# Attention and expert kernel on one core: finishing h from the maxima, gate divisors on GpSimd, and a new planned order

## The chip, the cores and the metric

The kernel runs on one core of one Trainium2 chip. The metric is the device time of one execution in microseconds. It was 238.63 us as the median of three runs, between 236.97 and 240.13.

## The reference, cut to what matters

There are 4 batches (B) of 11456 tokens (N) with 128 channels (C), and 32 inducing vectors (m). A first attention gathers each batch's tokens into 32 vectors h, a second one gives each token a mixture of its batch's h. Then every token is sent to one of 8 experts.

```python
scale = 1.0 / np.sqrt(C)
def mab(q, kv):
    s = scale * (q @ kv.transpose(0, 2, 1))
    s = s - s.max(-1, keepdims=True)
    a = np.exp(s)
    a /= a.sum(-1, keepdims=True) + 1e-09
    return a @ kv
h = mab(I, x)            # I: the inducing vectors, (B, 32, 128)
x = mab(x, h).reshape(B * N, 128)
xn = x / (np.linalg.norm(x, axis=-1, keepdims=True) + 1e-06)
logits = xn @ en.T / tau                 # en: 8 normalized expert vectors
expert_idx = np.argmax(logits, axis=1)
probs = softmax(logits)                  # with 1e-9 in the divisor
gate_w = probs[np.arange(N), expert_idx]
out = gate_w[:, None] * (relu(x @ w1[expert_idx]) @ w2[expert_idx])
```

## The kernel before, in words

**Stages.** A batch is cut into 6 pieces k: five of 2048 tokens and a last one of 1280 that laps over 64. All pieces of one batch go through these steps.

- `load_xT` and `load_x` (L382, L394) bring the piece in two layouts, channels by tokens (`xT`, 7 buffers; the last piece `xL`, 2) and tokens by channels (`x`, 6 half pieces). They are issued on SP's queue. For pieces 0, 1 and 3 of batch 0 the second layout is not loaded: `own` (L439) makes it on PE by transposes and copies it into a buffer of the output ring `o`.
- `stage1` (L462) is the first attention: scores on PE (L425), maximum over the row on DVE (L485), running maximum `nb` (L492, L494), exponentials on ACT (L500), the correction factor `fix` (L505), the running sum `zs` (L511), transposes on PE (L523), copies (L530), products with x on PE (L546) and the running h, `hj` (L556, L558). Batch 0 does it piece by piece, the others in pairs of pieces.
- `finish` (L562) makes h from them. The 128 partitions hold four groups of the 32 rows, each with a maximum of its own. The maxima are turned into one row (L570), their best per row is found (L575, L580), turned back (L584, L589), and gives a factor `fw` for each partition (L594); the sums are weighted with it (L600) and added over the groups (L604); from the inverse comes the matrix `sel` (L609 to L614), and one product with `hj` gives h transposed, `hT` (L620, L621, L626). `tables` (L680) makes what the gates need of h. Then the expert of the batch's h is picked (L639 to L646), and SP reads its index and loads that expert's two weight matrices (L674).
- `stage2` (L699) is the second attention for a piece: scores (L716), maximum over 32 rows (L722), spreading (L727), difference (L733), exponentials `e` (L738), a product for the squared norm (L744, copied at L750, multiplied on GpSimd at L754, summed at L758) and the products for the logits (L766, L767, turned at L774).
- `gate` (L780) takes three pieces together (the last batch 3, 2 and 1; nine gates in all): the norm's root on ACT, Newton's step on GpSimd (L825 to L828), the divisor `den` on DVE (L834, L835), logits on GpSimd (L840), their maximum (L845), subtraction (L849), exponentials on ACT (L854), their sum `se` on GpSimd (L864 to L866), the first maximum `v` on DVE (L871, L873), and `f` on DVE, the gate weight where the chosen expert is the batch's (L886 to L888). `zz` (L814) is the attention's own divisor.
- `fold` (L898) makes from the weights and h one matrix `L` per batch, which replaces the expert's two layers where no hidden unit changes its sign within the batch. `check` (L973) tests that.
- `stage3` (L1056) spreads `f` (L1042), weights `e` with it on GpSimd (L1046), multiplies with `L` on PE (L1065), copies to the output buffer `o` (L1072, 2 buffers) and stores it from ACT's queue (L373).
- `worklist` (L1098) lists what the tests left open; a loop at the end does that work in full. Its list is empty for these inputs.

**The order.** Nothing is scheduled by hand. Each step is an operation given to `Plan` (L102) with its engine, an estimated duration, what it depends on, which buffers and PSUM banks it takes and frees, and a due time `when`. `Plan.run` (L198) simulates the five engines in order: among the operations of an engine that can start within a margin (`NEAR`, L79) of the earliest it takes the one with the smallest `when` plus a correction by name (`FIRST`, L62; in the last batch also `LATE`, L70). Batch 0's first stage has due times below zero, then batch b's second stage runs with batch b+1's first. The order so found is the order in which the instructions are emitted; an engine works through its own in order, and so does a DMA queue. `HOP` is the assumed delay from one engine to another, `RATE` the assumed DMA rate in bytes per us.

**Zero products.** Where the plan sees PE idle for over 0.6 us before an operation that takes a bank, it puts products of zeros there (`fill`, L1153, its product in L1157), in that operation's own bank.

Of the kernel before, what the change touches and what calls it, by code (L numbers as in the profile page):

```python
# [44 lines left out]
NC = E + 1  # L45
# [16 lines left out]
FIRST = dict(G=-52.5, at=28.5, chk=-3, chosen=60, copy_s=47, den=23.5, diff=10, em=-60, evict=55.5, ex=-44, expA=21, expB=-30, expert=59,  # L62
             f=-59.5, fin=-58.5, first=-23, fix=8, flags=-11, fours=-5, fw=-44.5, gat=6, get_w=-10.5, get_x=53, get_xT=-48.5, gm=-38.5,
             gm4=-30, gmb=-12.5, good=-60, gv=-11.5, hT=8.5, hTc=-5.5, hb=-4.5, hj=55.5, hs=35.5, keep_e=23, keep_hq=-21, keep_x=-60,
             lg=-60, li=-16.5, lm=-47.5, mat=14.5, merge=8, mk=5, mults=-3, nb=51, newton=1, norm=-44, outs=34, parts=-21, pick=-47.5,
             pick_vals=46, places=39, prod=-2, put_h=54, put_li=-7.5, put_o=-30.5, r1=22, rm=60, root=8.5, root_e=23, rows=-5,
             score=-59.5, scores=-7, se=-2, seen=44, selr=-12, sides=-3, signs=52.5, some=-52, spread=-60, spread_f=14, square=-57.5,
             square_e=-9, squared=18.5, sums=4, times=36, top=58.5, turn=-31, turn_e=-52, turn_s=1.5, under=-37.5, vals=60, vp=-10.5,
             vpb=-14.5, weigh=60, zf=44, zs=38.5, zz=-60)
LATE = dict(G=1.5, L=-7, at=27.5, chk=48.5, chosen=-60, copy_s=60, den=14.5, diff=-31, em=35, evict=49.5, ex=34, expA=14, expB=1,  # L70
            expert=2.5, f=2.5, fin=-7, first=-60, fix=60, flags=-22.5, fours=56, fw=8, gat=28.5, get_w=60, get_x=21, get_xT=52, gm=56,
            gm4=60, gmb=-60, good=25, gv=-48.5, hT=-20, hTc=-31, hb=-60, hj=21, hs=52, keep_e=52.5, keep_hq=-58, keep_x=-43, lg=13.5,
# [1245 lines left out]
```

## Time and profile before

| what | value |
|---|---|
| median of three runs | 238.63 us |
| the profiled execution | 236.28 us |
| its span, first to last instruction | 234.5 us |
| mean granted TensorE clock | 0.905 |
| instructions | 5142 |
| busy PE, DVE, ACT, POOL | 198.0, 179.4, 118.2, 108.0 us |
| moved by DMA | 72.24 MB, 308 GB/s over the span |

The span is that of the instructions; 1.8 us of the profiled execution lie outside it. PE is TensorE's matrix product, PEld its loading of weights, DVE VectorE, ACT ScalarE, POOL GpSimd, SP the engine that issues most loads. "L754" is line 754 of the kernel. In a group of instructions, "hq<-hq,e" names the tile written and the tiles read; "x24" is the number of instructions. "A <- B" with a time is A's idle time until B released it. PE's busy time has modelled ends and overlaps in part, so a high share doesn't say that it works at its peak.

### The profile page before, as it was taken

The page shows a single profiled execution, that of the slowest core. Times are in us where ns is not written, and L with a number is a line of the kernel's source. Part 1 is how long each engine was busy: PE and PEld are TensorE (multiplying, and loading weights), DVE is VectorE, ACT ScalarE, POOL GpSimd, SP SyncE. Part 2 cuts the span into 40 slices and gives each one's busy share as a digit, 9 for nine tenths or more (in the row PEclk, how much of TensorE's full clock was granted, in tenths as well). Part 3 has the DMA queues.
Part 4 walks back from the last instruction along what each step waited for, and adds up shares of the span by engine and source line. Part 5 has one row for each costly group of instructions (what it writes and reads, how often), then busy time and mean ns, then how long its engine had stood idle before and what let it go on. Part 6 is the DMA issues. An engine that isn't in the chain of part 4 may idle for free.

```text
span 234.5 us, 5142 instructions
## 1 busy us (share of the span) xinstructions
PE 198.0 (84%) x1861; PEld 102.7 (44%) x1861; DVE 179.4 (76%) x512; ACT 118.2 (50%) x260; POOL 108.0 (46%) x172
## 2 busy tenths in 40 slices
PE   7799967999998789799988998998889989393730
PEld 2467526534655343445555524374533453151120
DVE  5455423989889797699989797698899899958740
ACT  2066504133835732267754363675753766568440
POOL 3000000054677660466579243765694466777710
PEclk9999997999999979999996799999976999859555
DMA  5999999699999779999989699994457094428483
GB/s 144 377 422 402 374 407 361 220 388 419 420 395 348 307 257 388 428 414 362 412 279 352 222 381 361 374 367 197 189 208 307 22 334 183 179 117 348 201 340 115
DMA packets 15230, 72.24 MB, mean 308 GB/s; under 512 B 2072, under 2 KB 2592, under 8 KB 10208
## 3 DMA queue, kind: packets, MB, share of 16 engines
q1 hardware_dynamic: 10816, 48.11, 53.6%
q10 hardware_dynamic: 4384, 23.76, 25.3%
q8 instruction: 16, 0.26, 0.5%
q14 instruction: 14, 0.11, 0.2%
HBM read 48.13 MB, written 23.72 MB: 306 GB/s over the span
## 4 chain that ended last, share of the span: by engine, by line


## 5 line engine op out<-in xcount | busy, mean ns | idle before, releaser
L754 POOL TENSOR_TENSOR hq<-hq,e 128x512 f32<-128x512 f32 (+1 forms) x24 | 29.0, 1211 | 69.0 <-ACT hq L750 69.0
L1072 ACT COPY o<-ps 128x512 f32<-128x512 f32 (+1 forms) x94 | 47.6, 569 | 20.4 <-PE ps L1065 14.0
L1065 PE MATMUL ps<-pf,L 32*128 32x512 f32 (+1 forms) x192 | 35.5, 736 | 6.6 <-POOL pf L1046 6.6
L1046 POOL TENSOR_TENSOR pf<-e,fb 128x512 f32<-128x512 f32 (+1 forms) x24 | 28.9, 1204 | 12.4 <-PE ps L1065 10.2
L425 PE MATMUL ps<-xT,indT_sb 128*32 128x512 f32 x160 | 21.2, 602 | 6.6 <-DMA xT<-in_xT 6.4
L744 PE MATMUL ps<-e,HB 128*128 128x512 f32 (+1 forms) x48 | 24.9, 609 | 0.3 <-DVE g L644 0.3
L738 ACT ACTIVATE e<-d 128x512 f32<-128x512 f32 (+1 forms) x24 | 14.5, 602 | 20.0 <-DVE R L733 18.8
L716 PE MATMUL ps<-xT,hT 128*32 128x512 f32 x160 | 23.1, 681 | 1.5 <-DVE hT L626 1.5
L750 ACT COPY hq<-ps 128x512 f32<-128x512 f32 (+1 forms) x24 | 13.4, 558 | 20.0 <-PE ps L744 14.6
L546 PE MATMUL ps<-x,pt 128*32 128x128 f32 x608 | 20.8, 287 | 0.2 <-ACT pt L530 0.2
L546 PEld LDWEIGHTS ps<-x,pt 128*32 128x32 f32 x608 | 17.2, 115 | 6.8 <-issue 2.7
L485 DVE TENSOR_REDUCE mk<-ps 128x1 f32<-128x1024 f32 (+3 forms) x15 | 14.1, 941 | 7.7 <-PE ps L425 7.3
L1065 PEld LDWEIGHTS ps<-pf,L 32*128 32x128 f32 x192 | 11.1, 218 | 16.3 <-POOL pf L1046 8.9
L722 DVE TRANSPOSE_TENSOR_REDUCE mx<-ps 128x16 f32<-128x512 f32 (+1 forms) x24 | 16.0, 667 | 2.1 <-PE ps L716 2.0
L727 DVE STREAM_TRANSPOSE mxb<-mx 128x512 f32<-128x512 f32 (+1 forms) x24 | 16.3, 678 | 0.8
L733 DVE CUSTOM_DVE_ANT_0 d<-mxb,ps 128x512 f32<-128x512 f32 (+1 forms) x24 | 15.4, 641 | 0.8
L1042 DVE STREAM_TRANSPOSE fb<-f 128x512 f32<-128x512 f32 (+1 forms) x24 | 15.4, 659 | 0.2
L766 PE MATMUL ps<-e,gbd 128*128 128x256 f32 (+1 forms) x48 | 15.0, 395 | 0.7 <-DVE R L733 0.7
L758 DVE TRANSPOSE_TENSOR_REDUCE nn<-hq 128x16 f32<-128x512 f32 (+1 forms) x24 | 15.4, 649 | 0.0
L500 ACT ACTIVATE s<-ps,nb 128x1024 f32<-128x1024 f32 (+3 forms) x15 | 13.4, 896 | 2.7 <-DVE nb L494 1.4
L523 PE MATMUL ps<-ident,s 128*128 128x128 f32 (+1 forms) x92 | 14.0, 292 | 0.8 <-ACT L L970 0.4
L767 PE MATMUL ps<-e,gbd 128*128 128x256 f32 (+1 forms) x48 | 13.9, 373 | 0.0
(189 smaller groups left out, 327.8 us busy)
## 6 DMA issues: line engine op xcount, KB each, us to landing
out<-o ACTq DMA_DIRECT2D x20, 1024.0 KB, 3.9
xT<-in_xT SPq DMA_DIRECT2D x19, 1024.0 KB, 9.9
x<-in_xP SPq DMA_DIRECT2D x38, 512.0 KB, 11.0
xL<-in_xT SPq DMA_DIRECT2D x4, 640.0 KB, 11.0
out<-o ACTq DMA_DIRECT2D x4, 608.0 KB, 3.9
w1t<-in_w SPq DMA_DIRECT2D x4, 512.0 KB, 4.8
w2t<-in_w SPq DMA_DIRECT2D x4, 512.0 KB, 6.2
xT<-in_xT SPq DMA_DIRECT2D x4, 256.0 KB, 4.5
```

The costliest lines, as they stand in the source:

```text
L425: nc.tensor.matmul(ps[32 * j:32 * j + 32, :].rearrange("p (g i) -> p g i", i=128), lhsT=indT_sb, rhs=v[:, j], start=True, stop=True)
L546: nc.tensor.matmul(ph.t[32 * j:32 * j + 32, 0:C], lhsT=pt.t[:tw, tat[k] + g, 32 * j:32 * j + 32], rhs=x, start=k == ks[0] and g == 0, stop ...
L716: nc.tensor.matmul(ps[32 * j:32 * j + 32, :W].rearrange("p (t i) -> p t i", i=32), lhsT=st.hT[:, 0:M], rhs=v[:, j], start=True, stop=True)
L722: nc.vector.tensor_reduce(new(mx)[:, :T], b1.t[:, :W].rearrange("p (t i) -> p t i", i=32), AX.X, ALU.max, apply_transpose=True)
L727: nc.vector.transpose(new(mxb)[:, :W], mx.t[:, :T].unsqueeze(2).broadcast_to([P, T, 32]))
L733: nc.vector.tensor_tensor_reduce(out=new(d)[:, :W], in0=mxb.t[:, :W], in1=b1.t[:, :W], scale=1.0, scalar=0.0, op0=ALU.subtract, op1=ALU.ma ...
L744: nc.tensor.matmul(new(b2)[:, :W], lhsT=st.HB, rhs=e.t[:, :W], start=True, stop=True)
L754: nc.gpsimd.tensor_tensor(paired(hq.t[:, :W]), paired(hq.t[:, :W]), halved(e.t[:, :W]), ALU.mult)
L758: nc.vector.tensor_reduce(new(nn)[:, t0:t0 + T], hq.t[:, :W].rearrange("p (t i) -> p t i", i=32), AX.X, ALU.add, apply_transpose=True)
L1046: nc.gpsimd.tensor_tensor(new(pf)[:, :W], st.e[k].t[:, :W], fb.t[:, :W], ALU.mult)
L1065: nc.tensor.matmul(new(pcs[j])[:, :W], lhsT=st.L[32 * j:32 * j + 32, :], rhs=pf.t[32 * j:32 * j + 32, :W], start=True, stop=True)
L1072: (nc.vector.tensor_copy if dve else nc.scalar.copy)(v[:, j], pcs[j].t[:, :W].rearrange("c (t i) -> c t i", i=32))
```

## The change

**h's finishing.** The first transpose (L570) depends on the last running maximum instead of the last `hj` and `zs`. The weighted sum depends on `zs`, and the product for h on `hj`:

```diff
-        c(PE, 0.2, fin, take=[b1], deps=st.do["A"])
+        c(PE, 0.24, fin, take=[b1], deps=[st.do["nb", len(ROWS[st.b]) - 1]])
...
-            nc.vector.tensor_tensor(t["z"], st.z1, t["fw"], ALU.mult)
-        c(DVE, 0.2, zf)
+            nc.scalar.activation(t["z"], st.z1, AF.Identity, scale=t["fw"])
+        c(ACT, 0.2, zf, deps=[st.do["A"][1]])
...
-        c(PE, 0.65, hT, take=[b4])
+        c(PE, 0.6, hT, take=[b4], deps=[st.do["A"][0]])
```

The running sum moves to ACT as well:

```diff
-                nc.vector.scalar_tensor_tensor(t, st.z1, v["fix"], v["z"], ALU.mult, ALU.add)
+                nc.scalar.activation(t, st.z1, AF.Identity, scale=v["fix"], bias=v["z"])
```

**Gates.** The product of the two divisors moves from DVE's `f` to GpSimd's `se` (in the last gate it stays on DVE), the comparison with the chosen expert becomes an instruction of DVE's `first`, the reciprocal an operation `inv` of its own, and `f` a product on GpSimd:

```diff
             nc.gpsimd.tensor_tensor(t["se"], x[:, :, 0], x[:, :, 1], ALU.add)
+            nc.gpsimd.tensor_scalar(t["se"], t["se"], 1.0, 1e-9, ALU.mult, ALU.add)
+            nc.gpsimd.tensor_tensor(t["se"], t["se"], t["zz"], ALU.mult)
...
             nc.vector.tensor_reduce(t["v"], t["lg"], AX.X, ALU.max)
+            nc.vector.tensor_scalar(t["v"], t["v"], st.vp, None, ALU.is_equal)
...
+        def inv():
+            nc.vector.reciprocal(t["se"], t["se"])
...
         def f():
-            nc.vector.scalar_tensor_tensor(t["se"], t["se"], 1e-9, t["zz"], ALU.add, ALU.mult)
-            nc.vector.reciprocal(t["se"], t["se"])
-            nc.vector.scalar_tensor_tensor(new(fv)[:, :T], t["v"], st.vp, t["se"], ALU.is_equal, ALU.mult)
+            nc.gpsimd.tensor_tensor(new(fv)[:, :T], t["v"], t["se"], ALU.mult)
```

**Loads and buffers.** Piece 0 of batch 0 is loaded by one DMA instead of four. The output ring has 3 buffers instead of 2. The temperature goes to 8 partitions instead of 128. A small table for the work list, `ax`, is loaded from SP's queue after the last batch's h and no longer at the start from ACT's. An unused constant, `nnb`, and its five memsets are gone.

**The plan.** All estimated durations are new. `HOP` goes from 0.2 to 0.07 with a lag per engine (PE 0.17, ACT 0.09, DVE 0.07, GpSimd 0.05), `RATE` from 390e3 to 405e3. The margins and corrections are new: `NEAR` is 0 for PE, ACT and DVE, 1 for SP and 0.1 for GpSimd, a table `HOLD` adds a margin by name (up to 2), and a table `START` adds corrections for what has due times below zero. `FIRST` and `LATE` have new values throughout. DVE operations marked `port` are held until GpSimd's current operation ends:

```diff
-        return max(t, o.room)
+        t = max(t, o.room)
+        return max(t, clock[POOL]) if o.port and self.pool_from < t else t
```

**Zero products.** They now go ahead of any PE operation before which the plan sees PE idle and a bank free for over 0.4 us, up to 16 instead of 12, in whichever bank is free soonest:

```diff
+    def spare_bank(self, o, a, b):
+        free = [(max(at, a), i) for i in range(BANKS) for at in [self.bank_at(i)] if at is not None]
+        at, i = min(free, default=(b, None))
+        return (i, b - at) if b - at > self.LEAST else None
...
-            if o.idle > self.LEAST:
-                self.fill(o.take[0], min(self.MOST, int((o.idle - self.SPARE) / self.FILL)))
+            if o.spare:
+                bank, idle = o.spare
+                self.fill(bank, min(self.MOST, int((idle - self.SPARE) / self.FILL)))
```

`SPARE`, the time kept back from such a gap, goes from 0.3 to 0.15.

More of the change, by code (lines that the diff above doesn't have):

```diff
@@ L44 @@
 ZC = E
-NC = E + 1
 ROOM = 1.0 - 1e-4
@@ L60 @@
 SLOT = 6
[L62 to L69, printed above, removed]
@@ new lines @@
+LATE = dict(G=53, L=-44, at=-25.5, chk=59, chosen=-43, copy_s=-8.5, den=-53.5, diff=53.5, em=7, evict=-48.5, ex=15.5, expA=33, expB=-10,
+            expert=19.5, f=-59.5, fin=-13, first=-27, fix=21, flags=44.5, fours=21, fw=-54, gat=47, get_ax=2, get_w=-46, get_x=-4.5,
+            get_xT=-33, gm=3, gm4=-32, gmb=48, good=-1.5, gv=1, hT=60, hTc=-8, hb=-27.5, hj=-55, hs=52, inv=24.5, keep_e=4, keep_hq=34,
+            keep_x=46, lg=-14, li=57.5, lm=-60, mat=32.5, merge=-23, mk=45, mults=-49, nb=60, newton=52, norm=57.5, outs=-1.5,
+            parts=-4.5, pick=22.5, pick_vals=-49.5, places=60, prod=18.5, put_h=-17, put_li=26.5, put_o=18.5, r1=-24, rm=60, root=-15,
+            root_e=-15.5, rows=-40, score=16.5, scores=18, se=-34, seen=44, selr=5.5, sides=60, signs=10.5, some=-17.5, spread=60,
+            spread_f=50.5, square=-19, square_e=10, squared=-46, sums=32, times=58, top=11, turn=-31, turn_e=44, turn_s=-19, under=-56,
+            vals=-60, vp=45.5, vpb=32, weigh=-21, zf=9.5, zs=-21, zz=-14.5)
@@ L125, in buf, with add @@
         return Buf(ring, n)
-    def add(self, eng, dur, fn, deps=(), when=0.0, take=(), free=(), size=0, after=0.0):
+    def add(self, eng, dur, fn, deps=(), when=0.0, take=(), free=(), size=0, after=0.0, port=False):
         o = Op()
@@ L215, in run @@
             o.start = t
-            o.idle = t - max(clock[o.eng], o.room) if o.eng == PE and o.take else 0.0
+            o.spare = self.spare_bank(o, clock[PE], t) if o.eng == PE else None
             clock[o.eng] = o.end = t + o.dur
+            o.done = o.end + o.lag
+            if o.eng == POOL:
+                self.pool_from = t
             if o.size:
                 dma = max(dma, o.end) + o.size / self.RATE
-                o.end = dma + self.LANDING
+                o.end = o.done = dma + self.LANDING
             for b in o.take:
@@ L390, in load @@
             return get_xT
-        st.do["xT", k] = [plan.add(SP, 0.45, load(a), take=[b] if a == 0 else [], when=when, size=w * P * 4) for a in range(0, n, w)]
+        st.do["xT", k] = [plan.add(SP, 0.36, load(a), take=[b] if a == 0 else [], when=when, size=w * P * 4) for a in range(0, n, w)]
     def load_x(plan, st, k, when):
@@ L589, in gmb @@
             nc.vector.tensor_copy(t["gmb"], b2.t[:, 0:1])
-        c(DVE, 0.2, gmb, free=[b2])
+        c(DVE, 0.1, gmb, free=[b2])
         def fw():
```

192 lines of the change are left out of this document (105 added, 87 removed).

## The prediction

> **What bounds the kernel now.** I read the busy time by stage first, cut at the moments when a batch's h is ready (41, 82.4, 128.6 and 175.4 us, rounded). Columns: stage, its length, then busy time (instructions) of PE, PEld, DVE, ACT and POOL, then TensorE's granted clock, DMA share, GB/s.
>
> ```profile
> 0.00:31.00 31.00, 27.12 (x332) 15.91 (x332) 15.43 (x77) 13.00 (x30) 1.94 (x12) 1.00 0.92 346
> 31.00:41.00 10.00, 7.24 (x47) 4.43 (x51) 3.19 (x12) 2.40 (x4) 0.00 (x0) 0.83 0.97 383
> 41.00:82.40 41.40, 39.22 (x418) 20.03 (x416) 36.78 (x95) 20.35 (x44) 22.21 (x33) 1.00 0.91 357
> 82.40:128.60 46.20, 42.69 (x434) 23.25 (x438) 40.96 (x108) 23.60 (x52) 25.76 (x40) 0.92 0.95 361
> 128.60:175.40 46.80, 42.86 (x427) 21.97 (x419) 39.58 (x104) 27.94 (x61) 26.25 (x38) 0.94 0.75 286
> 175.40:208.00 32.60, 27.38 (x159) 11.97 (x158) 30.18 (x76) 18.88 (x42) 20.09 (x31) 0.87 0.52 208
> 208.00:228.00 20.00, 11.45 (x60) 5.16 (x58) 13.24 (x44) 12.06 (x28) 11.74 (x20) 0.67 0.65 268
> 228.00:234.50 6.50, 0.00 (x0) 0.00 (x0) 0.00 (x0) 0.00 (x0) 0.00 (x0) 0.50 0.30 107
> ```
>
> Three regimes stand there. From 31 to 41 us almost nothing computes: DVE works 3.2 of 10 us, POOL not at all. From 41 to 208 us DVE is busy 147.5 of 167.0 us (88%) and PE 152.2 (91%): two engines share the bound. PE's number is flattering, since its ends are modelled and overlap. After 208 us there is a tail of dependent work on half-idle engines.
>
> The order of events between 25 and 41 us explains the hole (columns: start, duration, engine, line, operation; in brackets the idle time before and its releaser):
>
> ```profile
> 25.76 0.21 DVE L494 TENSOR_SCALAR nb<-mk,nb 128x1 f32<-128x1 f32 x1
> 27.83 0.22 DVE L511 SCALAR_TENSOR_TENSOR zs<-zs,fix,z 128x1 f32<-128x1 f32 x1 [1.18 <-ACT fix L505]
> 30.48 0.35 DVE L558 SCALAR_TENSOR_TENSOR hj<-hj,fix,ps 128x128 f32<-128x128 f32 x1 [1.33 <-PE ps L546]
> 31.07 1.06 PE L425 MATMUL ps<-xT,indT_sb 128*32 128x512 f32 x8 [0.66 <-DMA xT<-in_xT]
> 32.07 0.27 PE L570 MATMUL ps<-ident,nb 128*1 128x128 f32 x1
> 33.59 1.07 PE L425 MATMUL ps<-xT,indT_sb 128*32 128x512 f32 x8 [1.25 <-DMA xT<-in_xT]
> 34.59 0.38 PE L584 MATMUL ps<-ones,gm 1*128 1x1 f32 x2
> 36.11 0.29 ACT L594 ACTIVATE fw<-nb,gmb 128x1 f32<-128x1 f32 x1 [6.74 <-DVE gmb L589]
> 36.86 0.43 PE L604 MATMUL ps<-z,sel 128*128 128x1 f32 x2
> 37.91 0.29 DVE L614 TENSOR_SCALAR sel<-sel,selr 128x128 f32<-128x128 f32 x1
> 39.32 0.55 PE L620 MATMUL ps<-sel,hj 128*128 128x128 f32 x2
> 39.70 0.28 PE L621 MATMUL ps<-selr,hj 128*128 128x1 f32 x2
> 40.02 0.29 DVE L626 COPY hT<-ps 128x128 f32<-128x128 f32 x1 [1.82 <-PE ps L621]
> ```
>
> The last running maximum is there at 25.97 us and the last partial sum of h at 30.83. Yet the finishing starts only at 32.07, because it waits for both, and then its links on PE stand behind batch 1's scores, which wait for loads. h is ready at 40.31, 9.5 us after its last input. The same happens once per batch; for the last:
>
> ```profile
> 155.28 0.20 DVE L494 TENSOR_SCALAR nb<-mk,nb 128x1 f32<-128x1 f32 x1
> 166.87 0.35 DVE L558 SCALAR_TENSOR_TENSOR hj<-hj,fix,ps 128x128 f32<-128x128 f32 x1 [0.70 <-PE ps L546]
> 175.44 0.28 DVE L626 COPY hT<-ps 128x128 f32<-128x128 f32 x1
> ```
>
> Here 11.4 us lie between the maximum and the last sum, and 8.5 us more pass until h. DVE, however, is full in that stretch with the gates of the batch before (30.18 of 32.6 us in the stage that follows), so lateness costs there only what DVE runs dry of later.
>
> **The change, part by part.** The sum is made against the profiled execution: 234.5 us of span and 1.8 outside, 236.28 us. That is 2.35 us under the median of the three runs shown (238.63), so the median forecast is the sum plus 2.35.
>
> *h's finishing.* The first transpose now waits for the maximum alone, the factors' own sum for z, and only the final product for hj. By the rows the early links (0.27 + 0.38 + 0.29 + 0.43 + 0.29, and small DVE steps between) fit into the 4.9 us between 25.97 and 30.83, so after hj only 0.55 + 0.28 + 0.29 and the hops stay, about 1.5 us: h at 32.3, a gain of 8.0. If both scores still stand ahead of the product (33.59 + 1.07 = 34.66), h comes at 36.0, a gain of 4.3. The new planner believes in 405 GB/s where the stage shows 383, so it will send some score too early; I take 6.5.
>
> *First load in one piece, three output buffers.* The first score must have all four pieces anyway:
>
> ```profile
> 8.68 1.06 PE L425 MATMUL ps<-xT,indT_sb 128*32 128x512 f32 x8 [1.63 <-DMA xT<-in_xT]
> ```
>
> One issue instead of four puts the following loads behind the first sooner. The most that can be won is PE's 1.63 us of waiting; the least is nothing, or a loss of as much again if the single load lands later. I take 0.5. The third output buffer serves batch 0's transposed copies of x as well; it removes no more than a wait. So the start gives 7, with 3 and 10 as ends. The aux load moves off ACT's queue to SP's behind the last h, where no load follows but the item list; it is used at the very end, so it costs nothing unless it lands late.
>
> *Work off DVE.* Rows: busy in total, mean ns of one, idle before.
>
> ```profile
> L886 DVE SCALAR_TENSOR_TENSOR se<-se,zz 128x48 f32<-128x48 f32 (+3 forms) x9 | 6.1, 676 | 1.6 <-POOL se L866 1.5
> L888 DVE SCALAR_TENSOR_TENSOR f<-v,vp,se 128x48 f32<-128x48 f32 (+3 forms) x9 | 4.2, 472 | 0.3
> L511 DVE SCALAR_TENSOR_TENSOR zs<-zs,fix,z 128x1 f32<-128x1 f32 x7 | 2.4, 341 | 1.3 <-ACT fix L505 1.2
> L511 DVE SCALAR_TENSOR_TENSOR zs<-z,fix,z 128x1 f32<-128x1 f32 x4 | 0.7, 184 | 0.0
> L600 DVE TENSOR_TENSOR z<-zs,fw 128x1 f32<-128x1 f32 x4 | 1.4, 349 | 0.2 <-ACT fw L594 0.2
> L926 DVE TENSOR_SCALAR pos<-ss x4: 171/248/596, 51.1 to 198.4; 128x8 f32<-128x8 f32 x4
> L828 POOL TENSOR_TENSOR n<-n,p 128x48 f32<-128x48 f32 x4 | 1.1, 287 | 0.3
> L814 POOL TENSOR_SCALAR zz<-gts 128x48 f32<-128x48 f32 x4 | 1.1, 267 | 1.6 <-DVE gts L774 1.4
> L505 ACT ACTIVATE fix<-nb 128x1 f32<-128x1 f32 x11 | 3.2, 288 | 0.0
> POOL lg L840 <- DVE den L835: 7.9, 9, 1.6
> ```
>
> Off DVE go 6.1 + 4.2 + 2.4 + 0.7 + 1.4 = 14.8 us (for the last gate the divisor's product stays, 0.2). Added is one comparison per gate; its nearest row is L926 with 171, 248 and 596 ns as least, median and most, so 1.5 to 5.4 us in nine, and 2.2 at the median. Net 12.6, of which some 1.2 lie before 41 us: 11.4. The reciprocal stays on DVE as its own step. POOL gets eight times 267 + 287 and nine times 287, 7.0 us, beside 26 busy of 46 in a batch; ACT gets 15 activations of 288 ns at most, 4.3 us, beside 28 of 47. The new wait is f's, on POOL, for the reciprocal; behind it stand the products of L754 and L1046, and DVE's squares and PE's outputs wait for those. The like wait in the trace is POOL's for the divisor of L840, 7.9 us in nine, on an engine with that much to spare.
>
> What is 11.4 us off DVE worth? All of it if DVE alone were the bound, nothing if PE were (91% against 88%). With the two that close I take half less a little, 5, with 0 and 11.4 as ends.
>
> One rule speaks against this part. The Trainium skill, SBUF — State Buffer, section Who interferes with whom, says that DVE and GpSimd share a port pair as an exclusive lock, which a DVE instruction with two SBUF inputs can lose, and a `tensor_scalar` too. The trace agrees: L886 is slow by its mean. By the rule the added comparison would often pay its worst price, 596 ns, and the sum would stand 2 to 3 us higher, a bit more with POOL busier.
>
> *The new order.* It has no row. Idle between 41 and 208 us are 19.5 us of DVE and 14.8 of PE. With h ready about 6 us sooner in each batch some of that closes; priorities fitted to wrong durations can also open as much as they close. I take 2, with -6 and +8 as ends.
>
> *The tail.* After 208 us the chain is gate, weights, products, copies, store:
>
> ```profile
> 221.58 0.51 DVE L1042 STREAM_TRANSPOSE fb<-f 128x320 f32<-128x320 f32 x1
> 224.15 1.45 PE L1065 MATMUL ps<-pf,L 32*128 32x320 f32 x8
> 227.00 0.89 DVE L1072 COPY o<-ps 128x320 f32<-128x320 f32 x2 [0.15 <-issue]
> 166.74 0.82 PE L1065 MATMUL ps<-pf,L 32*128 32x320 f32 x8
> ```
>
> The last products take 1.45 us where the same shape takes 0.82 elsewhere, and DVE's copies wait until 227.00 behind the item list. A warm clock and a better order could give 0.6 and about 1; the last f now crosses to POOL and back, some 0.3 more. I take 1.5, with -1 and 4 as ends.
>
> Sum: 7 + 5 + 2 + 1.5 = 15.5; 236.28 - 15.5 = 220.8, and as a median 223.1 us.
>
> The Trainium skill, TensorE: Matmul & The Clock Gate, Part 1, says that TensorE is throttled to half unless it has been busy for some 3.4 us, so more zero products in gaps should lift the last stage; the clock of 0.67 and 0.50 there fits it. By that rule alone the tail would give its upper end and the time would be 2.5 us lower.
>
> **The rivals.**
> *Loads and PE keep the pace.* Between 41 and 128.6 us the DMA share is 0.91 and 0.95. Left idle are 0.09 x 41.4 + 0.05 x 46.2 + 0.3 = 6.3 us; if batch 2's and 3's h hang on loads, the start cannot give more than 6.3, and what leaves DVE counts only after 128.6 us, where about 5.4 of the 11.4 lie (69.8 of 147.5 busy us), half of it by PE: 2.7. Then 236.28 - 9.0 = 227.3, as a median 229.6. For it: the shares. Against it: shares of 0.75 and 0.52 later, so that most of the room for loads comes after that stretch.
>
> *The early finishing is not used.* hT still stands behind both scores on PE (gain 4.3), no order gain, and the gate's longer way over POOL takes back 3: 235.0, as a median 237.3. For it: PE is in order and the loads set those scores.
>
> *Zero products hold up PE (slower).* They now go ahead of any PE instruction for which the plan sees 0.4 us of idle time, into any bank that is free then. On the chip each still waits for that bank's last reader, and then runs.
>
> ```profile
> L1157 PE MATMUL ps<-wz 128*128 128x512 f16 x26 | 8.7, 456 | 2.0 <-DVE gmb L589 1.2 <-ACT o L1072 0.7
> ```
>
> Today there are 26 of 456 ns in the plan, mostly at the start, with 2.0 us of waits. On an engine that is busy 91% of its time, every one that the plan puts into a gap which isn't there costs about 0.4. It eats the whole 15.5 from 39 of them on; with 60 more the time is 236.28 - 15.5 + 24 = 244.8, as a median 247.1. Against it: they are sized to the plan's gaps less 0.15 us.
>
> **How the numbers follow.** Forecast (gain spread over start, DVE and order) 0.60; loads and PE keep the pace 0.20; not used 0.12; zero products 0.08. A measurement of this kernel tells about 2% from no change: below 233.9 us is faster, above 243.4 slower. The forecast and the first rival, but for a part of 0.03, are faster: 0.77. The second rival and that part: 0.15. The third: 0.08. The forecast's own range is 216 to 229: the ends of the terms seldom fall together. The range, 214 to 236, takes in the first rival and most of what lies between it and the second; beyond it are the slow rival, part of the second and a sum of all upper ends.
>
> **What would show it.** Right: the first transpose of the finishing right after the last maximum, h at 33 to 36 us, and POOL at work before 41 us; DVE's busy time near 167 us; stages between h's of 41 to 45 us. The first rival shows as unchanged distance of the second and third h from the loads, with a DMA share near 1 until 125 us. The second shows as hT behind two scores. The third shows as many zero products with PE waits ahead of them. I am wrong if DVE's busy time falls as said and the stages from 41 to 208 don't shrink, or if the new order opens waits of several us in one engine's queue.

## The result and the profile after

The changed kernel takes 215.44 us as the median of four runs (213.05 to 217.09), the kernel before beside it 239.0. The ratio is 0.899, with a 95% interval of 0.888 to 0.910: faster by a tenth. The forecast was 223.1, with 216 to 229 as its own range and 214 to 236 as the range of all cases. Medians here are of all runs, while ratios leave out runs in a slower state that some executions show, as the profiled one of the changed kernel does (217.09 us; the other three took 213.05 to 215.47).

The profiled execution took 217.09 us with a span of 215.4, so against the 236.28 of before 19.2 us are gone; 15.5 had been forecast. Its busy time by stage, cut at 31 us and then where each batch's h is ready, where the last gate weights are spread (L1077) and at the end; columns as in the prediction:

```profile
0.00:31.00 31.00, 28.88 (x320) 16.76 (x324) 14.51 (x70) 14.57 (x35) 1.89 (x11) 1.00 0.92 369
31.00:35.60 4.60, 4.52 (x51) 1.86 (x43) 2.48 (x10) 0.64 (x3) 0.00 (x0) 1.00 1.03 408
35.60:71.80 36.20, 35.39 (x401) 19.02 (x401) 30.95 (x82) 17.01 (x36) 15.75 (x23) 1.00 0.95 366
71.80:114.20 42.40, 39.50 (x412) 19.59 (x408) 38.69 (x97) 26.64 (x58) 27.05 (x49) 1.00 0.98 371
114.20:160.00 45.80, 42.93 (x462) 22.03 (x458) 38.98 (x109) 28.68 (x65) 29.25 (x48) 0.96 0.85 335
160.00:203.50 43.50, 39.77 (x251) 16.73 (x248) 40.22 (x110) 32.63 (x76) 37.06 (x63) 1.00 0.70 272
203.50:215.40 11.90, 5.18 (x34) 2.01 (x32) 3.24 (x17) 2.27 (x6) 2.12 (x5) 0.86 0.59 236
```

The hole from 31 to 41 us has shrunk to 4.6 us. The clock column stands at 0.96 to 1.00 up to the last spreading and at 0.86 after it, where before it fell to 0.50. With before cut in the same way, the stages compare so (us):

| stage | before | after | difference |
|---|---|---|---|
| start to first h | 40.3 | 35.6 | -4.7 |
| first to second h | 42.4 | 36.2 | -6.2 |
| second to third h | 46.2 | 42.4 | -3.8 |
| third to fourth h | 46.8 | 45.8 | -1.0 |
| fourth h to the last spreading | 46.4 | 43.5 | -2.9 |
| from there to the end | 12.4 | 11.9 | -0.5 |

The middle of both kernels, from first h to last spreading, as one row each. Before:

```profile
40.30:222.10 181.80, 161.60 (x1475) 81.72 (x1474) 157.74 (x410) 100.36 (x221) 104.75 (x158) 0.92 0.78 302
```

After:

```profile
35.60:203.50 167.90, 157.58 (x1510) 77.38 (x1511) 148.84 (x392) 104.96 (x234) 109.12 (x181) 0.99 0.86 334
```

The middle is 13.9 us shorter. DVE works 8.9 us less in it (157.74 to 148.84) and idles 5.0 less (24.1 to 19.1). That is an account, not yet a cause: it says where DVE's time went, not which edit made it so.

The finishing of batch 0's h, in the order of time:

```profile
27.62 0.21 DVE L523 TENSOR_SCALAR nb<-mk,nb 128x1 f32<-128x1 f32 x1
28.60 0.27 PE L599 MATMUL ps<-ident,nb 128*1 128x128 f32 x1
30.39 0.38 PE L613 MATMUL ps<-ones,gm 1*128 1x1 f32 x2
31.05 0.30 ACT L623 ACTIVATE fw<-nb,gmb 128x1 f32<-128x1 f32 x1
31.37 0.30 ACT L629 ACTIVATE z<-zs,fw 128x1 f32<-128x1 f32 x1
32.48 0.38 PE L633 MATMUL ps<-z,sel 128*128 128x1 f32 x2
32.67 0.35 DVE L587 SCALAR_TENSOR_TENSOR hj<-hj,fix,ps 128x128 f32<-128x128 f32 x1 [1.66 <-PE ps L575]
34.02 0.49 PE L649 MATMUL ps<-sel,hj 128*128 128x128 f32 x2
34.16 1.23 DVE L514 TENSOR_REDUCE mk<-ps 128x1 f32<-128x1024 f32 x1 [0.29 <-PE ps L454]
34.35 0.28 PE L650 MATMUL ps<-selr,hj 128*128 128x1 f32 x2
35.30 0.28 DVE L655 COPY hT<-ps 128x128 f32<-128x128 f32 x1
```

The chain now runs beside the last pieces: from the last `hj` (done at 33.02) to h (35.58) it takes 2.6 us where it took 9.5. Some 0.7 us of what is left is a maximum of batch 1 (L514) that stands ahead of the copy on DVE: the last product ends at 34.63, the copy begins at 35.30. In the other three batches `hj` to h is 1.1 to 1.7 us, where the last took 8.5. But the last `hj` itself comes 2.2 us later than before (30.83). The start of PE's work shows one reason:

```profile
8.66 1.91 PE L482 MATMUL ps<-ident,xT 128*128 128x128 f32 x16
10.50 1.06 PE L454 MATMUL ps<-xT,indT_sb 128*32 128x512 f32 x8
```

At 8.68 us the kernel before began with the first score; the new order puts 16 transposes ahead of it.

The end of the changed kernel:

```profile
203.05 0.50 DVE L1077 STREAM_TRANSPOSE fb<-f 128x320 f32<-128x320 f32 x1
203.30 1.74 POOL L1066 TENSOR_TENSOR seen<-seen 128x192 f32<-128x192 f32 x4
204.99 0.86 POOL L1081 TENSOR_TENSOR pf<-e,fb 128x320 f32<-128x320 f32 x1
205.91 0.82 PE L1100 MATMUL ps<-pf,L 32*128 32x320 f32 x8 [0.37 <-POOL pf L1081]
207.60 0.89 DVE L1107 COPY o<-ps 128x320 f32<-128x320 f32 x2
```

The same step of before:

```profile
220.93 1.74 POOL L1031 TENSOR_TENSOR seen<-seen 128x192 f32<-128x192 f32 x4
221.58 0.51 DVE L1042 STREAM_TRANSPOSE fb<-f 128x320 f32<-128x320 f32 x1
222.62 0.86 POOL L1046 TENSOR_TENSOR pf<-e,fb 128x320 f32<-128x320 f32 x1
```

The products take 0.82 us as hoped (1.45 before). But GpSimd merges the work list's counts (L1066, L1031 before; 1.74 us) ahead of the weighting. Before, this began 0.65 us ahead of the spreading, now 0.25 behind it, so `pf` begins 1.9 us after `fb` where it had been 1.0.

### The profile page after: what moved, and what is told of

The parts are those of the page before. It is cut to its first block, busy times and chain, and to the rows that moved or that the text cites. A ratio compares the mean times of both kernels' runs of the same rounds, so it can differ in the third digit from the quotient of the medians.

```text
span 215.4 us, 5252 instructions
## 1 busy us (share of the span) xinstructions
PE 196.2 (91%) x1909; PEld 98.0 (45%) x1909; DVE 169.1 (78%) x485; ACT 122.4 (57%) x275; POOL 113.1 (53%) x196
## 4 chain that ended last, share of the span: by engine, by line
PE 47%; DVE 24%; DMA 9%; POOL 7%; ACT 5%; issue 5%; ACTq 0%; DVEq 0%; POOLq 0%
DMA xT<-in_xT 9%; PE ps L575 7%; PE ps L454 6%; PE ps L1100 5%; PE ps L773 5%; PE ps L745 5%; PE ps L552 4%; DVE mk L514 3%; PE ps L1194 3%; POOL pf L1081 3%; PE ps L482 3%; PE ps L795 3%; DVE fb L1077 2%; PE ps L796 2%; DVE nn L787 2%
## 5 line engine op out<-in xcount | busy, mean ns | idle before, releaser
L1107 ACT COPY o<-ps 128x512 f32<-128x512 f32 (+1 forms) x94 | 47.7, 570 | 18.2 <-PE ps L1100 17.8
L1100 PE MATMUL ps<-pf,L 32*128 32x512 f32 (+1 forms) x192 | 27.4, 631 | 3.0 <-POOL pf L1081 1.7
L745 PE MATMUL ps<-xT,hT 128*32 128x512 f32 x160 | 20.8, 602 | 0.2
L1194 PE MATMUL ps<-wz 128*128 128x512 f16 x74 | 20.9, 414 | 0.0
L575 PEld LDWEIGHTS ps<-x,pt 128*32 128x32 f32 x608 | 15.7, 109 | 7.4 <-issue 2.7
L514 DVE TENSOR_REDUCE mk<-ps 128x1 f32<-128x1024 f32 (+3 forms) x15 | 14.2, 946 | 3.8 <-PE ps L454 2.7
L1077 DVE STREAM_TRANSPOSE fb<-f 128x512 f32<-128x512 f32 (+1 forms) x24 | 15.2, 655 | 0.9 <-POOL pf L1081 0.8
L756 DVE STREAM_TRANSPOSE mxb<-mx 128x512 f32<-128x512 f32 (+1 forms) x24 | 15.6, 655 | 0.2
L787 DVE TRANSPOSE_TENSOR_REDUCE nn<-hq 128x16 f32<-128x512 f32 (+1 forms) x24 | 15.5, 653 | 0.2
L1100 PEld LDWEIGHTS ps<-pf,L 32*128 32x128 f32 x192 | 8.5, 188 | 13.3 <-POOL pf L1081 6.8
## 6 DMA issues: line engine op xcount, KB each, us to landing
xR<-in_xR SPq DMA_DIRECT2D x4, 96.0 KB, 10.3
```

The costliest lines, as they stand in the source:

```text
L514: nc.vector.tensor_reduce(t, pc.t[:, :w], AX.X, ALU.max)
L575: nc.tensor.matmul(ph.t[32 * j:32 * j + 32, 0:C], lhsT=pt.t[:tw, tat[k] + g, 32 * j:32 * j + 32], rhs=x, start=k == ks[0] and g == 0, stop ...
L745: nc.tensor.matmul(ps[32 * j:32 * j + 32, :W].rearrange("p (t i) -> p t i", i=32), lhsT=st.hT[:, 0:M], rhs=v[:, j], start=True, stop=True)
L787: nc.vector.tensor_reduce(new(nn)[:, t0:t0 + T], hq.t[:, :W].rearrange("p (t i) -> p t i", i=32), AX.X, ALU.add, apply_transpose=True)
L1100: nc.tensor.matmul(new(pcs[j])[:, :W], lhsT=st.L[32 * j:32 * j + 32, :], rhs=pf.t[32 * j:32 * j + 32, :W], start=True, stop=True)
L1107: (nc.vector.tensor_copy if dve else nc.scalar.copy)(v[:, j], pcs[j].t[:, :W].rearrange("c (t i) -> c t i", i=32))
```

## The experiments

Every run below is a whole kernel; none leaves out a part of the computation. The zero products that some leave out have no reader. "Before" in a ratio is the kernel before on the same chip. The theory to test was that the 19 us are the sum of the terms of the prediction; the chief rival was that the order that was searched for these very operations carries them. The table gives the moments (us) at which h is there, the last spreading ends and the span ends, from each profile's rows of those two instructions.

| kernel | h 0 | h 1 | h 2 | h 3 | last spreading | span |
|---|---|---|---|---|---|---|
| before | 40.3 | 82.7 | 128.9 | 175.7 | 222.1 | 234.5 |
| after | 35.6 | 71.8 | 114.2 | 160.0 | 203.5 | 215.4 |
| after, late finishing, planned anew | 38.9 | 81.5 | 131.9 | 173.7 | 218.5 | 232.2 |
| after, late finishing, order held | 38.9 | 79.5 | 126.8 | 174.4 | 217.5 | 229.4 |
| before, early finishing, planned anew | 33.0 | 71.4 | 120.7 | 167.1 | 221.9 | 239.1 |
| before, early finishing, order held | 32.5 | 71.4 | 122.9 | 169.2 | 223.1 | 235.2 |
| after, priorities of before | 32.7 | 74.3 | 118.2 | 161.6 | 213.6 | 224.8 |
| the same, last batch with the new ones | 33.3 | 74.8 | 121.1 | 172.3 | 215.8 | 229.9 |
| after, planned for 402 GB/s | 33.9 | 73.2 | 116.0 | 160.0 | 207.8 | 220.1 |
| after, gate's divisors back on DVE | 35.6 | 71.6 | 113.1 | 156.3 | 200.5 | 211.9 |
| after, two output buffers, load in four | 35.2 | 71.4 | 113.1 | 163.3 | 208.1 | 222.5 |

### The finishing

**Late finishing in the changed kernel.**

```diff
-        c(PE, 0.24, fin, take=[b1], deps=[st.do["nb", len(ROWS[st.b]) - 1]])
+        c(PE, 0.24, fin, take=[b1], deps=st.do["A"])
```

> The changed kernel, planned anew, with the finishing of h again behind the last partial sum. Theory early finishing: each h comes 3 to 6 us later after its last sum, the start loses some 3 us and each boundary 1 to 2, 220 to 226 us. Rival: DVE and PE have other work in that time, and the plan moves it there; 214 to 218 us. A new plan alone may move the time by some us; another run measures that.

Measured: 234.18 us (233.39 to 234.73), ratio 0.988, 0.981 to 0.994. That is beyond the ranges of both theories: one dependency takes back nearly 19 of the 24 us. But `Plan.run` made a new order for it, so the run can't tell the wait from the loss of the searched order.

**The same with the order held.** The plan runs twice; in the second pass the priority of an operation is its start in the first, and only then the finishing waits. The order is held only in part: set side by side, with the zero products left out, the two traces have 446 of 1831 instructions on PE, 121 of 484 on DVE and 46 of 275 on ACT in another place; planned anew it was 843, 294 and 91.

```diff
+        if dry:
+            for o in order:
+                o.prio = o.start - getattr(o, 'bump', 0.0)
+                o.deps = getattr(o, 'deps2', o.deps)
...
-        c(PE, 0.24, fin, take=[b1], deps=[st.do["nb", len(ROWS[st.b]) - 1]])
+        o_f = c(PE, 0.24, fin, take=[b1], deps=[st.do["nb", len(ROWS[st.b]) - 1]])
+        o_f.deps2 = [*st.do["A"]]
...
+    plan.run(dry=True)
     order = plan.run()
```

> The changed kernel with its searched order held (each operation's start in the plan of the changed kernel becomes its priority in a second plan), and with the first step of h's finishing made to wait for h's last update again. Only the finishing chain and what must give way to it moves. Theory: the early finishing by itself is worth the three or so us that it takes off each batch's way to h at the start and part of it later, so 219 to 227 us, h of batch 0 at 39 to 41 us. Rival (the gain of 23 us is the searched order and the chain hardly counts): 214 to 218 us. Second rival (18 us of loss as in the run with late finishing under a new plan): 230 to 236 us.

Measured: 228.87, 231.33, 236.04 and 236.37 us, at mean granted clocks of 0.989, 0.976, 0.947 and 0.947; they lie too far apart for a ratio. Even the fastest is 13 us above the changed kernel's median, so the first rival (214 to 218) is out, and the theory's 219 to 227 was too low as well. Its stages:

```profile
0.00:38.90 38.90, 36.85 (x388) 20.64 (x388) 17.41 (x79) 17.19 (x40) 1.78 (x11) 1.00 0.95 375
38.90:79.50 40.60, 39.09 (x433) 20.83 (x436) 32.70 (x88) 19.62 (x45) 18.88 (x30) 1.00 0.86 334
79.50:126.80 47.30, 41.99 (x422) 20.76 (x418) 38.47 (x100) 25.97 (x56) 27.89 (x48) 0.96 0.88 342
174.40:217.50 43.10, 39.13 (x242) 16.42 (x235) 37.40 (x105) 27.09 (x61) 32.14 (x56) 1.00 0.55 217
```

The start loses 3.3 us, the next three stages 4.4, 4.9 and 1.8, the last batch nothing (43.1 against 43.5), where no later h waits. The DMA share falls from 0.95 and 0.98 to 0.86 and 0.88, which fits loads that wait for buffers a late h keeps taken: between the first and the third h the issues of `x` wait 34.5 us in sum for PE's products of stage 1 (23.5 in the changed kernel). So taking the early finishing out of this kernel costs far more than the 3.3 us at the start. How much of it is the wait, and how much an order that was searched for an early h and partly moved, isn't shown: no run gives the late finishing a searched order of its own.

**Early finishing in the kernel before**, planned anew: the three dependencies of the change, nothing else.

```diff
-        c(PE, 0.2, fin, take=[b1], deps=st.do["A"])
+        c(PE, 0.2, fin, take=[b1], deps=[st.do["nb", len(ROWS[st.b]) - 1]])
-        c(DVE, 0.2, zf)
+        c(DVE, 0.2, zf, deps=[st.do["A"][1]])
-        c(PE, 0.65, hT, take=[b4])
+        c(PE, 0.65, hT, take=[b4], deps=[st.do["A"][0]])
```

> The kernel before, planned anew with its own priorities, with only the dependencies of the finishing changed (maxima first; the running sum stays on DVE). Theory early finishing, as its undoing cost the changed kernel 19 us: 222 to 232 us, the first h near 36 us instead of 40.3. Rival, the gain needs priorities made for it, and undoing it only broke those: 234 to 241 us.

Measured: 240.36 us (238.57 to 244.38), ratio 1.006, 1.002 to 1.010. The four h come 7.3, 11.3, 8.2 and 8.6 us earlier, and nothing remains of it at the end. **With the order of before held**, and the finishing's operations moved up by 15 us:

```diff
+        o_f.deps2, o_f.bump = [st.do["nb", len(ROWS[st.b]) - 1]], 15.0
...
+        if o.name in ('gm', 'gm4', 'gmb', 'fw', 'zf', 'fin', 'selr', 'hT', 'hTc'):
+            o.bump = 15.0
```

> The kernel before with its own order held in the same way (a second plan whose priorities are the first plan's starts), and with the finishing chain freed to begin at the last comparison of the maxima and moved up by 15 us in the priorities. Theory (an earlier h is worth something once the rest of the order stays): 226 to 234 us, h of the batches 5 to 8 us earlier than before. Rival (as in the run with early finishing under a new plan, the four earlier h are given back in the last batch, which has more than one limit): 236 to 241 us, with the last batch over 50 us long from its h to its last final block.

Measured: 239.49 us (236.83 to 243.91), ratio 1.006, 0.998 to 1.013: the rival's case, with a last batch of over 50 us. Where the gain is given back:

```profile
32.50:71.40 38.90, 36.57 (x413) 20.13 (x414) 34.30 (x92) 19.01 (x41) 18.20 (x27) 1.00 1.02 403
71.40:122.90 51.50, 43.46 (x441) 22.73 (x441) 39.34 (x106) 24.86 (x53) 23.96 (x38) 0.93 0.84 323
169.20:223.10 53.90, 41.59 (x229) 17.96 (x221) 43.58 (x111) 31.96 (x73) 36.58 (x56) 0.88 0.54 217
```

Up to the second h the run is 11.3 us ahead of before. The next stage takes 5.3 us more (51.5 against 46.2), the last batch 7.5 more (53.9 against 46.4), of which DVE has 3.5 more work that the stages before left to it, and 4.0 more idle time. So the earlier h is real in both kernels, but only the changed one turns it into time. What is shown is that interaction, in an order that is again held only in part (355 of 1831 instructions on PE and 106 of 511 on DVE stand elsewhere). Of DVE's idle time in the last batch, 4.0 us stand ahead of the gates' `lg`, which waits there for ACT's exponentials (0.7 before); in the stage from second to third h, 3.8 and 2.2 us stand ahead of `gts` and `mx`, which wait for PE. No run shows what a change of these waits alone would give.

### The order

**The priorities of before in the changed kernel**: `FIRST`, `LATE` and `NEAR` of before, no `START` and no `HOLD`.

```diff
-FIRST = dict(G=-47.5, L=60, at=13.5, ...
+FIRST = dict(G=-52.5, at=28.5, chk=-3, ...
-START = dict(G=-273, ...
+START = dict()
```

> The changed kernel planned with the priorities and margins of the kernel before (its corrections by name in the first stage and the last batch, no table for the start, no margins by name), with the new durations. Theory order: the searched priorities carry most of the gain; 230 to 242 us. Rival: the parts carry it whatever the priorities; 215 to 226 us.

Measured: 228.32 us (226.47 to 230.36), ratio 0.960, 0.953 to 0.967. It has h at 32.7 us, 2.9 earlier than the changed kernel, and is still 1.6 behind at the fourth; the last batch then takes 52.0 us against 43.5. The time lies between the two theories' ranges. The searched priorities are worth 12.9 us to these operations.

**A control: the plan's DMA rate 0.7% lower**, which changes nothing but the order.

```diff
-    RATE = 405e3
+    RATE = 402e3
```

> A control: the changed kernel with the plan's DMA rate at 402 instead of 405 GB/s, so that the plan falls into another order while nothing of the work changes. If new plans are harmless, 213 to 218 us, and the 19 us of the late finishing are its own. If the priorities fit only the order that they were found for, 222 to 236 us, and the run with the late finishing says little about the finishing.

Measured: 222.46 us (222.42 to 224.31), ratio 0.935, 0.929 to 0.942. So this one disturbance of the plan costs 7 us. It is the only one measured, so it gives the grain of the experiments here that plan anew, not a bound: what they take away can be charged with some 7 us of lost fit.

**The new priorities in the last batch alone**, the old ones elsewhere.

```diff
-        o.prio = when + FIRST.get(o.name, 0.0) + (LATE if late else START if start else {}).get(o.name, 0.0)
+        o.prio = when + (FIRST2.get(o.name, 0.0) + LATE.get(o.name, 0.0) if late else FIRST.get(o.name, 0.0))
```

> The run with the old priorities (228.3 us), but with the new priorities for the operations of the last batch alone. Theory (the searched order earns its 13 us mostly in the last batch, which took 52.0 us there and 43.5 in the changed kernel): 217 to 222 us, last batch 43 to 46 us. Rival (the last batch is long because of the state in which the batches before leave the buffers and queues, so its own priorities don't mend it): 225 to 231 us.

Measured: 229.81 us (228.31 to 231.68), ratio 0.961, 0.954 to 0.969: no better than with the old ones throughout. Its last two stages:

```profile
121.10:172.30 51.20, 49.40 (x482) 24.42 (x481) 41.42 (x109) 35.91 (x78) 37.32 (x62) 1.00 0.81 314
172.30:215.80 43.50, 38.99 (x231) 16.25 (x230) 36.31 (x99) 24.39 (x58) 26.47 (x45) 0.99 0.51 202
```

Those of the run with the old priorities throughout:

```profile
118.20:161.60 43.40, 42.10 (x440) 21.80 (x440) 36.59 (x102) 29.60 (x65) 28.73 (x47) 1.00 0.84 325
161.60:213.60 52.00, 46.84 (x274) 18.74 (x274) 42.41 (x107) 31.26 (x71) 36.94 (x64) 1.00 0.53 211
```

The last batch falls to 43.5 us as the theory had it, and the stage ahead of it grows from 43.4 to 51.2. DVE's work changed places by the same amount (6.1 us out of the one, 4.8 into the other). A stage's length is thus no property of that stage: the two hold 95.4 and 94.7 us together. The theory that the last batch's own priorities earn the gain has fallen.

### The gates

**The gate's divisors back on DVE**, with their comparison and `f`.

```diff
-            nc.gpsimd.tensor_scalar(t["se"], t["se"], 1.0, 1e-9, ALU.mult, ALU.add)
-            nc.gpsimd.tensor_tensor(t["se"], t["se"], t["zz"], ALU.mult)
...
-            nc.vector.tensor_scalar(t["v"], t["v"], st.vp, None, ALU.is_equal)
...
+            nc.vector.scalar_tensor_tensor(t["se"], t["se"], 1e-9, t["zz"], ALU.add, ALU.mult)
             nc.vector.reciprocal(t["se"], t["se"])
...
-            nc.gpsimd.tensor_tensor(new(fv)[:, :T], t["v"], t["se"], ALU.mult)
+            nc.vector.scalar_tensor_tensor(new(fv)[:, :T], t["v"], st.vp, t["se"], ALU.is_equal, ALU.mult)
```

> The changed kernel in its own order, with the gate's instructions back on DVE in the places that the plan gives them: the product of the divisors ahead of the reciprocal, comparison and product in one where f stands. DVE's busy time rises by some 7 us (6.1 and 4.2 before, 3.5 for the comparison now), POOL's falls by 7. Theory DVE binds: about half of it or more shows, 219 to 224 us. Theory PE binds: nothing of it shows, 214 to 217 us. If POOL's added instructions delay its products more than they relieve DVE: under 214 us.

Measured: 213.61 us (213.47 to 217.29), ratio 0.901, 0.894 to 0.908. That is the changed kernel's time, and neither the 219 to 224 of the theory that DVE binds nor its 7 us of DVE's busy time came: the move is worth nothing that can be measured, and the kernel without it is no faster beyond doubt either. DVE's groups of that run show why:

```profile
L920 DVE SCALAR_TENSOR_TENSOR f<-v,vp,se 128x48 f32<-128x48 f32 (+3 forms) x9 | 3.6, 396 | 0.0
L915 DVE SCALAR_TENSOR_TENSOR se<-se,zz 128x48 f32<-128x48 f32 (+3 forms) x9 | 3.0, 333 | 0.0
```

In the changed kernel stands in their place:

```profile
L906 DVE TENSOR_SCALAR v<-v,vp 128x48 f32<-128x48 f32 (+3 forms) x9 | 3.5, 394 | 0.3
L891 DVE SCALAR_TENSOR_TENSOR se<-se,zz 128x10 f32<-128x10 f32 x1 | 0.6, 649 | 0.0
```

The divisors' product took 676 ns in the kernel before and takes 333 here, and `f` 396 for 472. Two of its instructions in the kernel before, with what GpSimd did beside them:

```profile
112.54 0.86 POOL L1046 TENSOR_TENSOR pf<-e,fb 128x320 f32<-128x320 f32 x1
112.61 0.85 DVE L886 SCALAR_TENSOR_TENSOR se<-se,zz 128x48 f32<-128x48 f32 x1
...
201.67 0.20 DVE L886 SCALAR_TENSOR_TENSOR se<-se,zz 128x48 f32<-128x48 f32 x1
201.69 1.31 POOL L754 TENSOR_TENSOR hq<-hq,e 128x512 f32<-128x512 f32 x1
```

The product that begins 0.07 us after GpSimd's ends 0.06 after it, and lasts 0.85 us; the one that begins just ahead of GpSimd's lasts 0.20. So a good part of the 6.1 us was waiting for GpSimd. In the new order six of the nine escape it (0.18 to 0.29 us). In the kernel before seven of the nine began after an instruction of GpSimd and ended 0.05 to 0.07 us behind it; the other two took 0.20 and 0.17. DVE's busy total is 169.3 us with the divisors and 169.1 without; two more runs with the changed kernel's instructions and order on DVE, those without zero products and with their old rule, have 166.9 and 168.1, so the move is worth between 0.2 and 2.4 us of busy time.

### The zero products

**None in the plan**; **the old rule** (over 0.6 us, the operation's own bank); **the new rule in the kernel before**.

```diff
-        for _ in range(n):
+        for _ in range(0):
             nc.tensor.matmul(ps_all[:, b]
```

> The changed kernel in its own order, but without any zero product of the plan (the four at the very start stay). Theory clock: a good part of the gain is that PE stays at full clock; the mean granted clock falls from 0.98 to 0.90 or less, PE's products in the tail go back to about 2.09 us for four of 512 columns, and the time rises to 222 to 232 us, a ratio to the kernel before of 0.93 to 0.97. Theory queues: the gain comes from h and from DVE's lighter load, and zero products only fill idle time; the time stays between 212 and 218 us, ratio 0.89 to 0.91, even if the clock falls. Third possibility, the slow rival of the prediction: they hold PE up, and without them the kernel is faster, under 211 us.

```diff
-    LEAST = 0.4
-    SPARE = 0.15
+    LEAST = 0.6
+    SPARE = 0.3
...
-            o.spare = self.spare_bank(o, clock[PE], t) if o.eng == PE else None
+            o.idle = t - max(clock[o.eng], o.room) if o.eng == PE and o.take else 0.0
```

> The changed kernel in its own order with the old rule of zero products (only ahead of operations that take a bank, in their own bank, over 0.6 us of idle time, at most 12). Theory clock: only the rule's reach matters; fewer zero products, clock between 0.90 and 0.96, 218 to 226 us. Theory queues: 213 to 217 us.

```diff
-    LEAST = 0.6
-    SPARE = 0.3
+    LEAST = 0.4
+    SPARE = 0.15
...
-            o.idle = t - max(clock[o.eng], o.room) if o.eng == PE and o.take else 0.0
+            o.spare = self.spare_bank(o, clock[PE], t) if o.eng == PE else None
```

> The kernel before in its own order, with the new rule of zero products. Theory clock: what leaving them out cost the changed kernel (220.7 us without any, 216.8 with the old rule) comes back here in part; the clock rises from 0.905 to 0.96 or more and the time falls by 2 to 6 us, to 232 to 236. Rival: the old order has its stalls elsewhere; the time stays between 236 and 240. Slow rival of the prediction: the products hold up PE, above 241.

Measured: 220.71 us (219.6 to 220.96; ratio 0.930, 0.924 to 0.937) without, 216.79 (216.23 to 218.4; 0.916, 0.908 to 0.923) with the old rule, and 236.5 (233.79 to 236.78; 0.988, 0.980 to 0.996) for before with the new rule. The order of the other instructions doesn't depend on them, and in the traces it is the same but for at most 2 instructions on PE, so these are clean: the new rule against none is worth 5.3 us, and 2 to 3 in the kernel before. Against the old rule it is 1.4, but there the intervals of the ratios overlap (0.888 to 0.910 and 0.908 to 0.923). The time without them lies between the two theories' ranges; with the old rule it is where the theory of queues had it and in the kernel before about where the rival had it, though the mean clock went as the theory of the clock said in both (0.940 for 0.984, and 0.969 for 0.905). Of the run without them, the last two stages:

```profile
160.80:205.00 44.20, 35.93 (x217) 15.21 (x213) 39.22 (x110) 31.19 (x73) 37.05 (x63) 0.85 0.66 259
205.00:217.70 12.70, 3.08 (x24) 1.64 (x20) 3.09 (x17) 3.61 (x8) 2.11 (x5) 0.63 0.62 249
```

The granted clock is 0.85 and 0.63 there, against 1.00 and 0.86 with them. The stages are 1.5 us longer together; of the 5.3 the profiles show 2.3 in the whole span (217.7 against 215.4), for the one execution lies 1.1 us below its kernel's median and the other 1.6 above. The group of the zero products in the changed kernel:

```profile
L1194 PE MATMUL ps<-wz 128*128 128x512 f16 x74 | 20.9, 414 | 0.0
```

74 stand where 26 were, and PE idled nowhere ahead of one.

### The third buffer and the load in one piece

**Two output buffers, first load in four pieces, order held.**

```diff
+    BUFS['o'] = 3
+    plan.run(dry=True)
+    BUFS['o'] = 2
     order = plan.run()
...
+        load_xT(plan, sts[0], k, EARLY * (k - 10), 4 if k == 0 else 1)
```

> The changed kernel with its order held, but with two output buffers and the first load in four pieces as before. Theory (neither is on the path: the first matmul of the changed kernel waits for all of the load, yet the start's later steps wait for the later loads, and the third buffer only spares waits on a port that has time): within 2 us of the changed kernel, 213 to 218 us. Rival (the store of an output takes 2 us, so copies into the third buffer run into it): 218 to 222 us, with idle time ahead of the copies of outputs that ends with a store.

Measured: 223.3 us (220.64 to 224.33), ratio 0.928, 0.920 to 0.937. By the medians that is some 8 us above the changed kernel, by the ratios 7; the theory of no effect has fallen, and the signs are the rival's. Its 2 us for a store are short: 1024 KB took 5.4 us in the changed kernel from issue to landing, at the median. The first three h come 0.4 to 1.1 us earlier than in the changed kernel, so the load isn't the cause. ACT near the end:

```profile
208.71 2.05 ACT L1119 COPY o<-ps 128x512 f32<-128x512 f32 x4 [1.51 <-DMA out<-o]
...
211.22 2.05 ACT L1119 COPY o<-ps 128x512 f32<-128x512 f32 x4 [0.47 <-DMA out<-o]
...
214.77 0.75 ACT L1119 COPY o<-ps 128x320 f32<-128x320 f32 x2 [1.49 <-DMA out<-o]
```

The copies wait for the store that empties their buffer, and the end grows from 11.9 to 14.4 us. Over the whole run such waits are 4.1 us on ACT and 1.1 on DVE; in the changed kernel no copy of outputs waits for a store. The other 5.7 us stand in the two stages before (50.2 and 44.8 us for 45.8 and 43.5). In the traces 111 of 1831 instructions on PE, 50 of 484 on DVE and 38 of 275 on ACT had changed places, because the plan sees the missing buffer too, so lost fit as in the control may be part of it. How much of the 8 us is the buffer by itself stays open, between the 2.5 of the end and all.

## Why the prediction was right, and where not

**The direction and the mechanism of the start** were right. The finishing begins right after the last maximum (28.60 after 27.62), and h is at 35.6 us, in the 33 to 36 that was to show it. Of the other signs, GpSimd begins stage 2 only at 42.4 us and not before 41 (47.7 before), and the stages between h's are 36.2, 42.4 and 45.8 us, of which the first and the last lie outside 41 to 45. The term was 7 and measured 4.7: the finishing gave 6.9, and stage 1 took 2.2 back, which the prediction hadn't priced. The run with the old priorities has h at 32.7 us with the same operations, so the delay is the new order's.

**Work off DVE** was right in its sum and wrong in its reason. DVE's busy time fell by 10.3 us to 169.1 (12.6 to 167 forecast); the comparison took 394 ns, between the 248 chosen and the 596 of the bad end. But the step "off DVE go 6.1 + 4.2" fails: putting them back costs DVE 0.2 to 2.4 us and the kernel nothing that can be measured. The long means, 676 and 472 ns, were read as work, while half of the first and more was waiting for GpSimd (333 ns are left in the new order, and 0.20 us is what one took that began first), so a new order takes much of it away without any move. The running sum and z, which really left for ACT, were 4.5 us of DVE. The Trainium skill, SBUF — State Buffer, section Who interferes with whom, has the two engines excluding one another at a shared port; the rule had been weighed only against the added comparison, at 596 ns. The trace agrees with the rule, with 0.20 us for the product that began first and 0.85 for the one that began after GpSimd's; it should have been weighed against the removed instructions first.

**The new order** is the step that failed in size. It was given 2, with 8 as its upper end. The searched priorities are worth 12.9 us on the same operations, 6 of them beyond the 7 that the control lost by a disturbed plan. The prediction treated it as a small correction to gains that stand by themselves. The runs show the reverse: put into the old order, early finishing gives nothing (ratio 1.006 in both runs); taken out of the new one, it costs 13 us or more with the order held in part and 19 planned anew. The terms don't add up: taking finishing, priorities, zero products and buffer away singly costs 19, 13, 5 and 8 us, 45 in all, where the whole change gave 24. Part of the 45 is lost fit, as in the control, so how the 24 us divide between finishing and order stays open.

**The tail** was given 1.5 and gave 0.5. The products became as short as said, and DVE's copy now stands ahead of the item list's last steps, 0.9 us after the products' end where it had been 1.4; the merge of counts on GpSimd (1.74 us) begins later against the spreading and takes 0.9 us of it back. What this step left out was GpSimd's own queue.

**Third buffer and load** were given 0.5 together, on the ground that a buffer "removes no more than a wait". Without it the end of the changed kernel is 2.5 us longer.

**The rivals.** *Zero products hold up PE* is refuted: there are 48 more, with 0.0 us of idle time ahead of them, and without any the kernel is 5.3 us slower. The forecast took no credit for their warmer clock beyond the tail's 0.6 us. The prediction's sentence from the Trainium skill (TensorE: Matmul & The Clock Gate, Part 1) would have given 2.5 us more, and the trace agrees in sign: the clock of the last batch's stage is 1.00 where the prediction's rows had 0.87 and 0.67. *The early finishing is not used* holds for the kernel before alone. In the changed kernel h's product on PE stands behind scores of batch 1 as well (the last of them from 33.03 to 34.09 us), but `sel`, which it needs, is there only at 33.88, so little is lost by it. *Loads and PE keep the pace* is refuted as a bound, though its signs are there: the DMA shares are 0.95 and 0.98 between the first and the third h, yet those stages lost 10.0 us, more than the 6.3 allowed. It took the bytes up to the third h as fixed. Before cut at the h:

```profile
0.00:40.30 40.30, 33.66 (x369) 19.73 (x369) 18.55 (x89) 15.07 (x34) 1.94 (x12) 0.96 0.94 359
40.30:82.70 42.40, 39.92 (x423) 20.64 (x422) 37.16 (x99) 20.68 (x45) 22.49 (x34) 1.00 0.90 354
82.70:128.90 46.20, 42.99 (x439) 23.53 (x443) 40.96 (x109) 23.60 (x52) 25.70 (x41) 0.92 0.95 361
```

By the rates at the rows' ends (GB/s) 359 x 40.3 + 354 x 42.4 + 361 x 46.2 = 46.2 MB had moved by the third h. After it is 369 x 31.0 + 408 x 4.6 + 366 x 36.2 + 371 x 42.4 = 42.3 MB: in the new order more of the traffic comes later, where the share had been 0.75 and 0.52.

So the time fell into the range near its lower end, with the sum short by 3.7 us in the profiled executions, and the order's term alone was short by about as much, if the control's 7 us are taken off its 12.9. That the sum came so near is in part luck: more than half of what it took off DVE was the gates' work, whose return costs nothing that can be measured, while the order's term was too small.

## What to carry to other kernels

A long mean of an instruction that other engines can hold up is no price of its work: see whether the same instruction is faster where they rest before paying for a move. In a kernel whose order is searched, an edit is worth what the order makes of it; measure it both ways, by taking it out of the new kernel and by putting it into the old one, and with a control that disturbs the plan alone, for here these gave 19, 0 and 7 us. A stage that gets shorter says little until the sum of it and its neighbours is seen.

## What was unexpected of the hardware

The running sum on ACT takes 387 ns for one number per partition, where the activation with one such operand less takes 296:

```profile
L540 ACT ACTIVATE zs<-zs,z,fix 128x1 f32<-128x1 f32 x7 | 2.7, 387 | 0.1
L629 ACT ACTIVATE z<-zs,fw 128x1 f32<-128x1 f32 x4 | 1.2, 296 | 0.1
```

The prediction had bounded both by the 288 ns of `fix`. The Trainium skill, ScalarE: Activation LUTs, section What ACT_TABLE_LOAD costs, gives 186 ns plus about 93 for each operand with one number per partition, by which an estimate for the first is 373 ns; the trace agrees, and the rule had not been used. How strictly DVE waited for GpSimd was not expected either: 0.85 us for a product of 48 numbers per partition that takes 0.20 when it begins first, up to the end of GpSimd's instruction. And a drop of the granted clock to 0.85 and 0.63 in the last stages without zero products went with only 1.5 us more in them by the two profiles, though with 5.3 between the medians. DVE stays the busier engine in the first of these stages (39.2 us against 35.9 of PE); that this is why is not shown.
